# One score group more in a pair, exponentials two by two, and other slots for two batches' side steps

## The chip, the cores and the metric

The kernel runs on one core of a Trainium2 chip. The metric is the time of one execution on the device, in microseconds (us), as the median of several runs. TensorE (PE in the rows, its weight loads PEld) multiplies matrices, ScalarE (ACT) applies functions, VectorE (DVE) and GpSimd (POOL) work elementwise, SyncE (SP) issues most DMAs. Each engine works off its own list of instructions in order; engines wait for one another through semaphores that the language sets.

## The reference

Attention over 4 batches of 12 heads (448 positions, head size 64) with a cap on the scores feeds a mixture of experts: each of the 1792 rows goes to the one expert, of 8, that its gate picks.

```python
scores = scale * q @ k.T                        # per batch and head, 448 x 448
scores = cap * tanh(scores / cap)
attn = exp(scores - max);  attn = attn / (sum(attn) + 1e-9)
x = (attn @ v)  as rows                         # 1792 x 768
logits = x @ w_gate;  e_idx = argmax(logits)
gate_w = softmax(logits)[e_idx];  eom = sigmoid(x @ w_output_gate)
out[rows of e] = gate_w * eom[:, e] * (relu(x[rows of e] @ w1[e]) @ w2[e])
```

## The kernel before, in words

The work has two stages: attention, which ends some 215 us into the profiled execution, and the experts. The change is in the first, and the second is left as it was.

Two heads of a batch are a pair; there are 24 pairs, numbered u = 0 to 23, six to a batch. The loop over u (from line 863) writes for each pair, in this order, what each engine gets:

- `qk(u, s)`, s = 0 to 3: the scores of one block of positions, into one of two PSUM buffers named s. Blocks 0 to 2 are full groups: three products (the high and low parts of k and q, tiles KH, KL, QH, QL), each as two matmuls, one for each head, side by side on the two halves of TensorE's rows. Block 3 is the half group: the 64 remaining positions of both heads as three matmuls on all rows. Behind each group ScalarE applies tanh (line 303, into a tile th, of which there are three).
- The exponential of a group (line 285, into the pair's tile pt) is not put on ScalarE's list with its tanh but one group later: `pend_exp` holds it, and `flush_exp()` in the next `qk` releases it. So tanh and exponential alternate.
- `pv(u - 1, c)`, c = 0 to 3: the previous pair's exponentials times v, into the PSUM tile u (lines 317 and 320).
- `presum(u, .)`: GpSimd adds up a pair's exponentials in three steps (lines 328, 329 and, as two half adds, 333). `sums(u)`: for every other pair TensorE sums them over positions with four matmuls (line 352, tile sm).
- `u_evac` copies a finished pair's result out of PSUM, and `prep(u + 2)` transposes a later pair's k and q (lines 272 and 259, tiles tk and tq), which VectorE then splits into high and low parts.

Between these stand the calls `slot(u, s)` for s = 0, 1, 2, 2.5 and 3. A slot runs the side steps that were put there. When a batch's six pairs are done, its side steps (`end_of_batch`) are spread over the next batch's pairs by the table `at`, whose key x counts slots from pair 6(b+1)+1: x = 5 is slot 1 of the pair after that one, x = 6 its slot 2, and so on. The side steps are: `gate_mm`, `gate_out` (the gate's products on TensorE, lines 389, copied out by ScalarE, line 395, in two halves t[2] and t[3]); `sums_out` (ScalarE copies the sums, line 367, tile ssb); `sums_tr`, `recips` (transposes trec, then VectorE's reciprocals rec, line 377); `gts`, two steps of transposes pg (line 404) and a product by rec (line 411); `logits` and `choose` (VectorE: the best expert); `rank_mm`, `place`, `place2` (TensorE's trk, then VectorE: each row's place in its expert's list); `enter` (VectorE, and then four indirect DMAs from GpSimd, line 474, that scatter the batch's entries into the tables tab); and the six row steps `rws` (transposes trow of one pair, line 483, scaled by VectorE, line 487, and stored to DRAM by a DMA on SyncE's queue, line 490).

All these transposes and products share two PSUM buffers (tag t) with tk and tq: each waits until the buffer of the one before the last has been read.

The batches b = 0 and 1 use one table; batch 2 has its own, with more in a slot, because the experts' first blocks are chosen from it: behind its `enter` come `early`, the weights' first loads, and `gather(0)`, with which the experts begin. Batch 3's steps run in the experts' stage.

Of the kernel before, what the change touches and what calls it, by code (L numbers as in the profile page):

```python
# [21 lines left out]
def tile_kernel(ctx: ExitStack, tc, q, k, v, cap, w_gate, w_ogate, w1, w2, out):  # L22
    nc = tc.nc
    B, H, S, D = q.shape
# [257 lines left out]
    def flush_exp():  # L282
        while pend_exp:
            dst, th = pend_exp.pop(0)
            nc.scalar.activation(out=dst, in_=th, func=ACTF.Exp, scale=capc)  # L285

    def qk(u, s):
        KH, KL, QH, QL = pl[u]
        if s == 0:
            pt[u] = ptp.tile([128, 2 * NK + 1, S], F32, tag="pt", name="pt")  # L290
        n = 2 if s < NK else 1
        sl = slice(s * 128, (s + 1) * 128)
        ps = ps_s.tile([128, 2, 512], F32, tag="s", name="s")
        if s < NK:
            for i, (x, y) in enumerate(((KH, QH), (KL, QH), (KH, QL))):
                for j in range(2):
                    h = slice(64 * j, 64 * j + 64)
                    nc.tensor.matmul(ps[:, j, 0:S], lhsT=x[h, sl], rhs=y[h], start=(i == 0), stop=(i == 2))  # L298
        else:
            for i, (x, y) in enumerate(((KH, QH), (KL, QH), (KH, QL))):  # L300
                nc.tensor.matmul(ps[:, 0, 0:S], lhsT=x[:, sl], rhs=y, start=(i == 0), stop=(i == 2))
        th = thp.tile([128, 2, S], F32, tag="th", name="th")
        nc.scalar.activation(out=th[:, 0:n], in_=ps[:, 0:n, 0:S], func=ACTF.Tanh, scale=icap)  # L303
        flush_exp()
        pend_exp.append((pt[u][:, 2 * s:2 * s + n], th[:, 0:n]))

    def pv(u, c):
        P = pt[u]
        V = vvs[u % 3]
        if c == 0:  # L310
            if u < NU - 1:
                ups[u] = ps_u.tile([128, S], F32, tag="u", name="u")
            else:
                ups[u] = ps_s.tile([128, 2, 512], F32, tag="s", name="u")[:, 0, 0:S]
        if c < NK:
            for j in range(2):
                nc.tensor.matmul(ups[u][64 * j:64 * j + 64], lhsT=V[:, c, j, :], rhs=P[:, 2 * c + j],  # L317
                                 start=(c == 0), stop=False)
        else:
            nc.tensor.matmul(ups[u], lhsT=V[:, c].rearrange("p j d -> p (j d)"), rhs=P[:, 2 * c], start=False, stop=True)  # L320
# [43 lines left out]
    def end_of_batch(b):  # L364
# [130 lines left out]
        rws = [L(P(row_tr, p), P(row_out, p)) for p in range(NP)]  # L495
        t = [sums_out, L(sums_tr, recips), L(P(gate_mm, 0), P(gate_out, 0)), L(P(gate_mm, 1), P(gate_out, 1))]
        gts = [L(P(gate_tr, g), P(gate_mul, g)) for g in range(2)]
        if b < B - 2:
            at = {1: [t[2]], 2: [sums_out], 5: [t[3], t[1]], 6: [rws[0], gts[0]], 10: [rws[1], gts[1]], 11: [logits],
                  12: [choose], 14: [rws[2]], 18: [rank_mm, place, rws[3]], 21: [place2], 23: [enter], 22: rws[4:6]}  # L500
        elif b == B - 2:
            g = early()
            nx = P(next, g, None)
            lds = [P(load_raw, 0, w, c) for w in range(2) for c in range((KD, KF)[w])]
            fd = [P(fetch_dma, i) for i in range(NE)]
            at = {-1: [sums_out], 1: [t[2], t[3]], 2: [t[1], *gts], 3: [logits], 4: [choose],
                  6: [rws[0]], 6.5: [rank_mm, place, place2, enter]}
            for i, x in enumerate(RWP, 1):
                at.setdefault(x, []).append(rws[i])
            for i, x in enumerate(NXP):  # L510
                at.setdefault(x, []).append(nx)
            at[8] = lds[:EL]
            for x, fs in ((9, [fd[0], P(set_known, NE), fd[1]]), (15, [P(gather, 0), fd[2]]), (16, [P(gather, 1), fd[3], *lds[EL:]])):
                at.setdefault(x, []).extend(fs)
# [338 lines left out]
    EARLY = (B - 1) * NP - 1  # L853

    def slot(u, s):
        for f in slots.pop(4 * u + s, ()):
            f()

    for u in range(NU):
        if u > 2:  # L860
            load(u + 3)
        qk(u, 0)
        qk(u, 1)
        if u > 0:
            presum(u - 1, 1)
        slot(u, 0)
        if u > 0:
            pv(u - 1, 0)
            pv(u - 1, 1)
        slot(u, 1)  # L870
        if u in (1, 2):

            prep(u + 1)
            load(u + 3)
        qk(u, 2)
        if u == 0:
            prep(1)
            load(3)
        else:
            pv(u - 1, 2)  # L880
        if u > 1 and u - 2 != EARLY:
            sums(u - 2)
        slot(u, 2)
        qk(u, 3)
        if u > 0:
            pv(u - 1, 3)
            u_evac(u - 1)
        slot(u, 2.5)
        if u > 1:
            prep(u + 2)  # L890
        if u - 1 == EARLY:
            sums(u - 1)
        load_v(u + 2)
        presum(u, 0)
        slot(u, 3)
    u = NU - 1
# [338 lines left out]
```

## Time and profile before

| | us |
|---|---|
| median of 3 runs | 535.86 (535.81 to 539.33) |
| the profiled execution | 536.26 |
| its span in the trace | 534.6 |
| TensorE busy in the span | 512.5 |
| ScalarE | 381.4 |
| VectorE | 339.2 |
| GpSimd | 300.2 |

The page of the profile gives busy time by engine and the costliest groups of instructions. The timeline gives single instructions: start, length, engine, line, what is written from what, and in brackets the idle time of the engine before it and what released it. Matmuls are pipelined and the ends of their rows are modelled, so on TensorE the distance from one row's start to the next is read, not the length. The windows give busy time and TensorE's granted clock (1.00 is full speed, 0.50 half) for chosen stretches. Line numbers are those of the kernel before; from line 304 on the changed kernel's are one higher.

### The profile page before, as it was taken

Reading aid. Unit: us, or ns where it says so; the run is one execution under the profiler, and the core shown is the slowest. Engines: PE = TensorE matmul, PEld = TensorE weight load, DVE = VectorE, ACT = ScalarE, POOL = GpSimd, SP = SyncE. Lnnn points to the kernel's source line nnn. Section 1 sums busy time; section 2 is a strip of 40 time slices with the busy share of each in tenths; the row PEclk is TensorE's granted clock in tenths of the full one; section 3 lists DMA queues with packets and bytes.
Section 4 is the critical chain, followed back from the end, with each engine's and each line's share of the span. In section 5 each row is a group of like instructions: output and inputs, shape, how many; then the busy total and the mean of one; then the engine's idle time right before and its main releaser. Section 6 shows DMA issues by size and latency. Waiting matters only on the chain. (4 is left out here: it accounts for less than half of the span.)

```text
span 534.6 us, 10384 instructions
## 1 busy us (share of the span) xinstructions
PE 512.5 (96%) x3197; PEld 360.2 (67%) x3197; DVE 339.2 (63%) x574; ACT 381.4 (71%) x498; POOL 300.2 (56%) x343
## 2 busy tenths in 40 slices
PE   7999999999999989789999999999999899999993
PEld 6555455555555544367999888887888768676691
DVE  3353356745674783979998896885767766545440
ACT  5988978887888689635678887886767857565550
POOL 8988777877887679725254964314556043331001
PEclk9999999999999899999999999999999999999997
DMA  6653334453445247787159526339759879891001
GB/s 146 141 117 89 87 87 104 103 126 85 103 105 121 52 76 222 260 286 199 61 204 385 215 92 227 107 85 408 240 170 399 321 273 389 281 359 72 1 30 49
DMA packets 106190, 91.95 MB, mean 172 GB/s; under 512 B 80770, under 2 KB 88970, under 8 KB 106128
## 3 DMA queue, kind: packets, MB, share of 16 engines
q1 hardware_dynamic: 97392, 58.48, 37.5%
q0 software_dynamic: 8736, 32.74, 17.1%
q8 instruction: 27, 0.44, 0.3%
q14 instruction: 35, 0.29, 0.2%
HBM read 123.68 MB, written 12.04 MB: 254 GB/s over the span
## 5 line engine op out<-in xcount | busy, mean ns | idle before, releaser
L947 DVE TENSOR_TENSOR wr<-raw,wr 128x768 fp32r<-128x768 f32 (+1 forms) x167 | 171.7, 1067 | 67.1 <-ACT wr L946 59.3
L946 ACT ACTIVATE wr<-raw 128x768 fp32r<-128x768 f32 (+1 forms) x167 | 150.2, 935 | 30.1 <-PE py L968 9.5
L303 ACT ACTIVATE th<-s,icap 128x896 f32<-128x896 f32 x96 | 87.3, 911 | 33.7 <-PE s L298 17.8
L285 ACT ACTIVATE pt<-th,capc 128x896 f32<-128x896 f32 x96 | 90.3, 942 | 0.0
L968 PE MATMUL py<-wr,hh 128*128 128x384 f32 x352 | 77.3, 340 | 0.0
L968 PE MATMUL php<-wr,xh 128*128 128x512 f32 x264 | 74.7, 404 | 0.0
L1037 POOL DMA_INDIRECT out_dram<-yo,ti x13 | 18.1, 1390 | 93.2 <-ACT yo L1035 87.1
L317 PE MATMUL u<-pt,vv 128*64 128x448 f32 x288 | 64.5, 556 | 0.0
L968 PEld LDWEIGHTS py<-wr,hh 128*128 128x128 f32 x352 | 61.2, 188 | 4.0 <-issue 3.7
L328 POOL TENSOR_TENSOR pa<-pt 128x896 f32<-128x896 f32 x23 | 48.4, 2103 | 17.0 <-ACT pt L285 12.2
L968 PEld LDWEIGHTS php<-wr,xh 128*128 128x128 f32 x264 | 47.5, 188 | 12.2 <-issue 2.5
L333 POOL TENSOR_TENSOR pb<-pb,pt 64x448 f32<-64x448 f32 x44 | 50.2, 1141 | 9.5 <-DMA tab<-ent,posi 5.2
L329 POOL TENSOR_TENSOR pb<-pa,pt 128x896 f32<-128x896 f32 x23 | 48.8, 2122 | 4.5 <-POOL pa L328 1.8
L968 PE MATMUL py<-wr,hl 128*128 128x384 f32 x176 | 44.8, 335 | 0.0
L968 PE MATMUL php<-wr,xl 128*128 128x512 f32 x132 | 41.5, 395 | 0.0
L1084 POOL DMA_DIRECT2D rh<-in_moe_w_dram x42 | 23.5, 562 | 24.4 <-DVE wr L947 14.2
L340 DVE COPY ut<-u 128x448 f32<-128x448 f32 x19 | 11.9, 624 | 37.4 <-PE u L320 31.0
L317 PEld LDWEIGHTS u<-pt,vv 128*64 128x64 f32 x288 | 16.5, 135 | 26.4 <-issue 21.2
L298 PE MATMUL s<-QH,KH 64*128 64x448 f32 x144 | 31.7, 437 | 2.3 <-ACT pt L285 1.1
L968 PEld LDWEIGHTS py<-wr,hl 128*128 128x128 f32 x176 | 31.8, 188 | 0.0
L487 DVE TENSOR_TENSOR xr<-trow,rec 112x512 f32<-112x512 f32 x24 | 16.1, 685 | 21.2 <-PE trow L483 18.1
L968 PEld LDWEIGHTS php<-wr,xl 128*128 128x128 f32 x132 | 24.7, 187 | 6.1 <-DVE xl L761 0.2
(243 smaller groups left out, 846.1 us busy)
## 6 DMA issues: line engine op xcount, KB each, us to landing
raw<-in_moe_w_dram SPq DMA_DIRECT2D x78, 512.0 KB
raw<-in_moe_w_dram SPq DMA_DIRECT2D x104, 384.0 KB
rh<-in_moe_w_dram POOLq DMA_DIRECT2D x18, 512.0 KB
rh<-in_moe_w_dram POOLq DMA_DIRECT2D x24, 384.0 KB
lq<-in_q_dram SPq DMA_DIRECT2D x24, 224.0 KB
kk<-in_k_dram SPq DMA_DIRECT2D x24, 192.0 KB
vv<-in_v_dram SPq DMA_DIRECT2D x24, 192.0 KB
xs<-xr SPq DMA_DIRECT2D x18, 224.0 KB
```

Of the source, the lines that this page charges most:

```text
L285: nc.scalar.activation(out=dst, in_=th, func=ACTF.Exp, scale=capc)
L298: nc.tensor.matmul(ps[:, j, 0:S], lhsT=x[h, sl], rhs=y[h], start=(i == 0), stop=(i == 2))
L303: nc.scalar.activation(out=th[:, 0:n], in_=ps[:, 0:n, 0:S], func=ACTF.Tanh, scale=icap)
L317: nc.tensor.matmul(ups[u][64 * j:64 * j + 64], lhsT=V[:, c, j, :], rhs=P[:, 2 * c + j], start=(c == 0), stop=False)
L328: eng.tensor_tensor(out=a, in0=P[:, 0:2], in1=P[:, 2:4], op=ALU.add)
L329: eng.tensor_tensor(out=s1[u], in0=a, in1=P[:, 4:6], op=ALU.add)
L333: eng.tensor_tensor(out=s1[u][h, j], in0=s1[u][h, j], in1=P[h, 2 * NK], op=ALU.add)
L946: nc.scalar.activation(out=t[:, 0, 0:F], in_=raw, func=ACTF.Copy)
L947: nc.vector.tensor_tensor(out=t[:, 1, 0:F], in0=raw, in1=t[:, 0, 0:F].bitcast(F32), op=ALU.subtract)
L968: nc.tensor.matmul(ps[g][:, 0:n], lhsT=st[:, c], rhs=w[:, z, g * n:(g + 1) * n], start=(c == 0 and st is hi and z == 0), stop=(c == (KD, K ...
L1037: nc.gpsimd.indirect_dma_start(out=out, out_offset=bass.IndirectOffsetOnAxis(ap=ti, axis=0), in_=y, in_offset=None, bounds_check=NT - 1, o ...
L1084: nc.gpsimd.dma_start(out=d, in_=src[bass.ds(e, 1)].rearrange("e (k p) f -> p (e k) f", p=128)[:, c], **kw)
```

## The change

It has three parts. First, `flush_exp` now runs only behind the odd groups, s = 1 and s = 3: ScalarE's list has two tanhs, then their two exponentials. Second, in the loop `pv(u - 1, 2)` and `sums(u - 2)` are moved from behind `qk(u, 2)` to the place behind `pv(u - 1, 1)`, so that the half group `qk(u, 3)` follows `qk(u, 2)`, with slot 2 between the two. Third, the table of batches 0 and 1 is written anew: both halves of the gate in one slot, the steps `gts` in slot 1 of their pairs and no longer beside a row step in slot 2, and logits, choose, rank, place and enter some slots later; the last row step of batch 0 has a slot of its own in the next batch's first pair.

```diff
--- before.py
+++ after.py
@@ -301,8 +301,9 @@
                 nc.tensor.matmul(ps[:, 0, 0:S], lhsT=x[:, sl], rhs=y, start=(i == 0), stop=(i == 2))
         th = thp.tile([128, 2, S], F32, tag="th", name="th")
         nc.scalar.activation(out=th[:, 0:n], in_=ps[:, 0:n, 0:S], func=ACTF.Tanh, scale=icap)
-        flush_exp()
         pend_exp.append((pt[u][:, 2 * s:2 * s + n], th[:, 0:n]))
+        if s % 2:
+            flush_exp()
 
     def pv(u, c):
         P = pt[u]
@@ -496,8 +497,9 @@
         t = [sums_out, L(sums_tr, recips), L(P(gate_mm, 0), P(gate_out, 0)), L(P(gate_mm, 1), P(gate_out, 1))]
         gts = [L(P(gate_tr, g), P(gate_mul, g)) for g in range(2)]
         if b < B - 2:
-            at = {1: [t[2]], 2: [sums_out], 5: [t[3], t[1]], 6: [rws[0], gts[0]], 10: [rws[1], gts[1]], 11: [logits],
-                  12: [choose], 14: [rws[2]], 18: [rank_mm, place, rws[3]], 21: [place2], 23: [enter], 22: rws[4:6]}
+            at = {1: [t[2], t[3]], 2: [sums_out], 5: [t[1]], 6: [rws[0]], 9: [gts[0]], 10: [rws[1]], 13: [gts[1]], 14: [rws[2]],
+                  15: [logits], 16: [choose], 18: [rws[3]], 21: [rank_mm, place], 22: [rws[4]], 23: [place2], 24: [enter]}
+            at.setdefault(26 if b < B - 3 else 22, []).append(rws[5])
         elif b == B - 2:
             g = early()
             nx = P(next, g, None)
@@ -867,6 +869,9 @@
         if u > 0:
             pv(u - 1, 0)
             pv(u - 1, 1)
+            pv(u - 1, 2)
+        if u > 1 and u - 2 != EARLY:
+            sums(u - 2)
         slot(u, 1)
         if u in (1, 2):
 
@@ -876,10 +881,6 @@
         if u == 0:
             prep(1)
             load(3)
-        else:
-            pv(u - 1, 2)
-        if u > 1 and u - 2 != EARLY:
-            sums(u - 2)
         slot(u, 2)
         qk(u, 3)
         if u > 0:
```

On TensorE, in pair 4 (tile s are the scores, u the products with v; 64x448 is one head's matmul); lines with - are before, with + after:

```order
 L298 MATMUL s<-QL,KH 128x448 x2
-L317 MATMUL u<-pt,vv_128 64x448 x4
-L298 MATMUL s<-QH,KH 128x448 x2
-L298 MATMUL s<-QH,KL 128x448 x2
-L298 MATMUL s<-QL,KH 128x448 x2
-L317 MATMUL u<-pt,vv_128 64x448 x2
-L301 MATMUL s<-QH,KH 128x448
-L301 MATMUL s<-QH,KL 128x448
-L301 MATMUL s<-QL,KH 128x448
-L320 MATMUL u<-pt,vv_128 128x448
+L318 MATMUL u<-pt,vv_128 64x448 x6
+L298 MATMUL s<-QH,KH 128x448 x2
+L298 MATMUL s<-QH,KL 128x448 x2
+L298 MATMUL s<-QL,KH 128x448 x2
+L301 MATMUL s<-QH,KH 128x448
+L301 MATMUL s<-QH,KL 128x448
+L301 MATMUL s<-QL,KH 128x448
+L321 MATMUL u<-pt,vv_128 128x448
```

The scores stood in three stretches of a pair, parted by products; now they stand in two. Where slot 2 holds a row step, its four transposes stand between the two score groups.

On ScalarE, in pair 13, where batch 1's gate (gsb) and sums (ssb) are copied out; th is a tanh, pt an exponential. Before:

```order
L303 ACTIVATE th<-s,icap 128x896
L285 ACTIVATE pt<-th,capc 128x448
L303 ACTIVATE th<-s,icap 128x896
L285 ACTIVATE pt<-th,capc 128x896
L395 ACTIVATE gsb_1571<-tg 128x448
L303 ACTIVATE th<-s,icap 128x896
L285 ACTIVATE pt<-th,capc 128x896
L367 ACTIVATE ssb<-sm 128x448
L303 ACTIVATE th<-s,icap 128x448
L285 ACTIVATE pt<-th,capc 128x896
```

and now:

```order
L303 ACTIVATE th<-s,icap 128x896 x2
L285 ACTIVATE pt<-th,capc 128x896 x2
L396 ACTIVATE gsb_1570<-tg 128x448
L396 ACTIVATE gsb_1575<-tg 64x448
L303 ACTIVATE th<-s,icap 128x896
L368 ACTIVATE ssb<-sm 128x448
L303 ACTIVATE th<-s,icap 128x448
L285 ACTIVATE pt<-th,capc 128x896
L285 ACTIVATE pt<-th,capc 128x448
```

The second half of the gate came a pair later; now all three copies stand ahead of the pair's last tanh.

On GpSimd, at the scatter of batch 0 (pa and the first pb are a pair's full adds, the pb of 64x448 its two half adds). Before:

```order
L328 TENSOR_TENSOR pa<-pt 128x896
L329 TENSOR_TENSOR pb<-pa,pt 128x896
L474 DMA tab_108<-ent,posi 15488x2
L474 DMA tab_109<-ent,posi 15488x2
L474 DMA tab_110<-ent,posi 15488x2
L474 DMA tab_111<-ent,posi 15488x2
L333 TENSOR_TENSOR pb<-pb,pt 64x448 x2
L328 TENSOR_TENSOR pa<-pt 128x896
```

and now:

```order
L329 TENSOR_TENSOR pa<-pt 128x896
L330 TENSOR_TENSOR pb<-pa,pt 128x896
L334 TENSOR_TENSOR pb<-pb,pt 64x448 x2
L475 DMA tab_108<-ent,posi 15488x2
L475 DMA tab_109<-ent,posi 15488x2
L475 DMA tab_110<-ent,posi 15488x2
L475 DMA tab_111<-ent,posi 15488x2
L329 TENSOR_TENSOR pa<-pt 128x896
```

The scatter stood ahead of pair 12's half adds; now it stands behind them, ahead of pair 13's first full add. Batch 1's moves in the same way, from pair 18's half adds to pair 19's first add. Batch 2's stays where it was, ahead of pair 20's first add.

## Rows read from the trace of the kernel before

**Rows 1.** The page: its first line.

```profile
span 534.6 us, 10384 instructions
```

**Rows 2.** Windows: stretch, length, busy time and count by engine, granted clock, DMA.

```profile
300.00:400.00 100.00, 100.00 (x732) 84.40 (x731) 74.48 (x84) 74.94 (x101) 49.63 (x65) 1.00 0.51 178
...
177.20:180.50 3.30, 3.30 (x15) 2.49 (x15) 1.73 (x3) 1.70 (x3) 3.12 (x2) 0.50 0.17 39
```

**Rows 3.** Timeline, TensorE, pair 6: start, length, line, tiles, count.

```profile
52.35 0.47 PE L298 MATMUL s<-QH,KH 64*128 64x448 f32 x2
53.06 0.37 PE L298 MATMUL s<-QH,KH 64*128 64x448 f32 x2
...
53.77 1.72 PE L317 MATMUL u<-pt,vv 128*64 128x448 f32 x8
55.43 0.47 PE L298 MATMUL s<-QH,KH 64*128 64x448 f32 x2
...
56.23 0.97 PE L317 MATMUL u<-pt,vv 128*64 128x448 f32 x4
57.13 0.47 PE L301 MATMUL s<-QH,KH 128*128 128x448 f32 x1
...
57.85 0.91 PE L320 MATMUL u<-pt,vv 128*128 128x448 f32 x2
```

**Rows 4.** The page's costliest groups: busy, mean ns; idle before, releaser.

```profile
L303 ACT ACTIVATE th<-s,icap 128x896 f32<-128x896 f32 x96 | 87.3, 911 | 33.7 <-PE s L298 17.8
...
L328 POOL TENSOR_TENSOR pa<-pt 128x896 f32<-128x896 f32 x23 | 48.4, 2103 | 17.0 <-ACT pt L285 12.2
...
L333 POOL TENSOR_TENSOR pb<-pb,pt 64x448 f32<-64x448 f32 x44 | 50.2, 1141 | 9.5 <-DMA tab<-ent,posi 5.2
```

**Rows 5.** Timeline, ScalarE, start of pair 6 (in brackets: idle before, releaser).

```profile
53.33 1.01 ACT L303 ACTIVATE th<-s,icap 128x896 f32<-128x896 f32 x1 [0.82 <-PE s L298]
```

**Rows 6.** Timeline, TensorE's weight loads, third score group of pair 6.

```profile
55.43 0.19 PEld L298 LDWEIGHTS s<-QH,KH 64*128 64x128 f32 x2 [0.70 <-ACT pt L285]
```

**Rows 7.** Timeline, TensorE: pair 0, and pair 10's row step.

```profile
10.69 0.66 PE L272 MATMUL tk<-ident,kk 128*128 128x128 f32 x4
11.18 0.55 PE L259 MATMUL tq<-ident,lq 112*128 112x112 f32 x4
...
92.58 0.65 PE L483 MATMUL trow<-ident,ut 128*112 128x128 f32 x4
92.99 0.45 PE L301 MATMUL s<-QH,KH 128*128 128x448 f32 x1
```

**Rows 8.** Timeline around pair 14's start: GpSimd, ScalarE, TensorE.

```profile
120.37 1.17 POOL L333 TENSOR_TENSOR pb<-pb,pt 64x448 f32<-64x448 f32 x1
...
121.62 0.64 ACT L303 ACTIVATE th<-s,icap 128x448 f32<-128x448 f32 x1 [0.97 <-PE tq L259]
...
122.31 0.47 PE L298 MATMUL s<-QH,KH 64*128 64x448 f32 x2 [0.63 <-ACT th L303]
```

**Rows 9.** Timeline in pair 19: GpSimd, TensorE, VectorE.

```profile
171.19 0.95 POOL L474 DMA_INDIRECT tab<-ent,posi  x1 [0.30 <-issue]
172.45 0.96 POOL L474 DMA_INDIRECT tab<-ent,posi  x1 [0.30 <-issue]
...
172.84 0.92 PE L404 MATMUL pg<-ident,gsb 128*112 128x128 f32 x4
...
174.68 0.30 DVE L377 TENSOR_SCALAR rec<-trec,epsc 112x48 f32<-112x48 f32 x1 [6.30 <-PE pg L404]
...
175.04 0.96 PE L404 MATMUL pg<-ident,gsb 128*112 128x128 f32 x4 [1.27 <-DVE rec L377]
```

**Rows 10.** Timeline, from the third scatter to the first expert's transposes.

```profile
189.88 0.96 POOL L474 DMA_INDIRECT tab<-ent,posi  x1 [4.65 <-DVE KL L253]
...
212.88 0.19 POOL L737 TENSOR_TENSOR tc<-tc 128x4 f32<-128x4 f32 x1
...
220.00 0.85 PE L759 MATMUL pt_x<-ident,xg 128*128 128x128 f32 x6 [3.03 <-DMA xg<-xs,ti]
```

## The prediction, made before the result was known

> **What bounds the kernel now.** I read the page first for the span, 534.6 us [rows 1]; the profiled execution took 536.26 us, so 1.66 us lie around the span, and it stands 0.4 us above the median of the runs, 535.86. Then the windows: in the experts' stage TensorE is busy in all 100.00 us of 300 to 400 [rows 2]. What attention gains is carried to the end, as long as the experts can start earlier by as much.
>
> Then TensorE's timeline in one plain pair, 6 [rows 3]. The reader is to see starts that follow one another without a hole, in stretches of scores and stretches of products: TensorE bounds this pair by the length of its list. ScalarE does not: it stands 33.7 us idle ahead of its tanhs, and scores end most of these waits [rows 4]; at pair 6's start it waits 0.82 us [rows 5]. So with the exponentials two by two ScalarE runs the same operations and nothing is gained by that itself.
>
> **The change, part by part.**
>
> *Regrouping on TensorE.* From the starts in [rows 3]: a full score group that ends a stretch takes 53.77 - 53.06 = 0.71, one that begins a stretch takes 53.06 - 52.35 = 0.71, and one that stands alone takes 56.23 - 55.43 = 0.80. Beginning or ending a stretch therefore costs 0.09 each. Two product groups take 55.43 - 53.77 = 1.66, one alone 57.13 - 56.23 = 0.90, so one more behind two costs 0.76, and a stretch of its own 0.14. Before, a pair's middle is score, product, half group, each alone. Now the third product stands behind the first two, and the half group behind the third score group. That saves 0.14 + 0.09 + 0.09 = 0.32 in a pair where slot 2 is empty.
>
> What the saving rests on is seen in the weight loads: at the turn from products to scores the load starts at 55.43, when its matmul starts, after 0.70 idle [rows 6]; it isn't ahead of it. The Trainium skill (TensorE: Matmul & The Clock Gate, Step-by-step: what each phase is for) has the next weights pulled ahead under the running matmul; by that alone turns would be free and this part would save 0. The row differs at these turns, and I go by the row; the other end is a rival below.
>
> Pairs 1 to 6 and 7 have nothing on TensorE in slot 2: 7 x 0.32 = 2.24. In pairs 8 to 20, 13 of them, slot 2 holds row steps, in pair 19 the transposes of sums and gate. There the two score groups stay apart and 0.14 is left, less what the transposes lose by standing behind scores instead of products. Behind products a row step takes 92.99 - 92.58 = 0.41; behind scores the four transposes of pair 0 take 11.18 - 10.69 = 0.49 [rows 7]. These have more columns (128 against 112), so 0.49 bounds the row step from above; from below it is 0.41. A turn of 0.14, as for products, is the far end: 0.55. I take 0.47, nearest the transposes, and 0.08 saved: 13 x 0.08 = 1.04, between 0 and 1.82.
>
> *The products moved ahead.* The third product now needs the pair before's third exponential 0.8 us earlier, but that exponential no longer waits for the next pair's first tanh. It is done early in the pair, where the product starts 3.1 us into it (0.71 + 0.71 + 1.66). This costs nothing. If its cover were gone, it would cost the rest of one exponential. The sums need GpSimd's adds of two pairs ago, a whole pair old: nothing.
>
> *ScalarE.* The score buffer of `qk(u, 2)` waits for the pair's first tanh, that of `qk(u, 3)` for the second. Both now run back to back, and are over three operations of some 0.91 [rows 4] after the start of the first, 0.98 into the pair [rows 5]: by 3.7 us at most, while TensorE comes to `qk(u, 2)` at 0.71 + 0.71 + 1.66 + 0.76 = 3.84. Of the four operations behind them only the tanhs hold TensorE. In pairs 7, 13 and 19 the gate's copies stand ahead of the third tanh (in 7 and 13 the sums' copy too), and wait for the gate's products. ScalarE falls behind by up to three short operations there, and TensorE then needs the third tanh only at the next pair's start, some 3 us after its scores: nothing, or at most 0.6 once or twice.
>
> *The gate's steps.* Moved, not changed: the gate's second half from pair 8 to 7 (14 to 13), the transposes pg from slot 2 to slot 1. They follow products in both places: 0. The row steps' DMAs stay in slot 2, ahead of the next v load on SyncE's queue, as before; batch 0's last moves one pair on, with no reader for 80 us. VectorE's steps move with it, off the path: 0.
>
> *The scatters.* Behind the fourth scatter of a batch two engines stand still. In pair 14 the half add behind it ends at 120.37 + 1.17 = 121.54, ScalarE's last tanh of pair 13 starts at 121.62 and TensorE loses 0.63 [rows 8]. In pair 19 the fourth scatter starts at 172.45; the transposes trec are over when pg starts, at 172.84; VectorE takes them up at 174.68 only. The second pg starts at 175.04, 2.20 after the first, and 1.27 of it idle, as its row says [rows 9]. TensorE then runs from 177.20 to 180.50 with half the clock granted, all 3.30 us of it busy [rows 2]: 1.65 lost. So pair 19 lost 1.27 + 1.65 = 2.92, and pair 14 0.63.
>
> Now both scatters stand behind a pair's half adds, 2 x 1.14 later in GpSimd's list [rows 4], but the exponentials that these adds wait for come earlier. Worked out for pair 19: pair 18's second exponential ends 4.8 into it, its third by 7.3, the adds (2.1 each, half adds 2 x 1.14) are over at 11.7, and pair 18, its steps added up, is about 8.8 long, so the scatters start 2.9 into pair 19, 172.45 - 171.19 = 1.26 apart, and the fourth at 6.7. TensorE reaches trec's end at about the same 6.7. It was 0.39 behind the fourth's start before. That is a margin of 0.4: VectorE has taken up trec before the still stretch, or has not. I take it that it has. For pair 13 the still stretch falls on its last transposes, which wait for no one: 0.63 goes as well.
>
> *Sum.* 2.24 + 1.04 + 0.63 + 2.92 = 6.83; 536.26 - 6.83 = 529.4. Pairs 21 to 23 count for nothing: from the third scatter at 189.88 GpSimd works off its adds up to 212.88, then the first gather, for which TensorE waits 3.03 until 220.00 [rows 10]. What counts is how much earlier pair 20's rank comes.
>
> **The rivals.**
>
> 1. *The margin in pair 19 fails:* the still stretch catches trec again, with the slow clock behind it. For it: 0.4 us is less than I can work out. Then 529.4 + 2.9 = 532.3 (531 to 534).
> 2. *Turns save nothing:* the 0.14 and 0.09 turn up elsewhere, in loads that then stand alone, and only the two stalls go: 536.26 - 0.63 - 2.92 = 532.7. Against it: the late load in [rows 6]. It is the case that the rule above describes.
> 3. *The gain is swallowed at the change of stages:* the wait of 3.03 [rows 10] grows by what attention saves, because something that isn't moved holds the gather: 535.9 to 536.3. Against it: scatter, rows and fetch all follow pair 20's rank.
> 4. *Slower:* the still stretch lasts as long as GpSimd's next operation. In [rows 8] both end together. Behind the moved scatters stands a full add, 2.10, instead of a half add, 1.14 [rows 4]: 0.96 more in pairs 13 and 19. Each would then cost 1.27 + 0.96 + 1.65 = 3.9, both 7.8, and if the clock stays low for two such stretches 5.5 each, 11.0. Against a gain of 2.24 + 1.04 + 0.63 + 2.92 = 6.83 this gives 537.2 to 540.4. It turns slower where the two places cost over 3.4 each. Against it: ScalarE, which has no part in that add's tiles, was held too, so the add alone isn't the cause.
>  The Trainium skill (SBUF — State Buffer, Who interferes with whom) says that a VectorE instruction with two SBUF inputs is fully blocked until a GpSimd one that reads SBUF is over, and that one with at most one such input is not. By it rec, which reads PSUM, would not be held by an add at all, and this rival would fall; the rows show it held, and don't tell by what.
>
> **Numbers.** The forecast of 529.4 has a chance of 0.45 (its own range 527 to 531.5), rival 1 0.27, rival 2 0.10, rival 3 0.09, rival 4 0.09. The range 526.5 to 536.2 takes in the first three and part of the fourth; rival 4 is left out. A measurement of this kernel can tell about 1%, 5.4 us, from no change: faster means under 530.5. That is most of the forecast's case and a little of rivals 1 and 2: 0.44. Slower by over 1%, above 541.2, is the tail of rival 4: 0.04. The rest is 0.52.
>
> **What would show it.** Right: in a plain pair the half group starts some 0.7 behind the third score group, and plain pairs are 0.32 shorter; pg's second step follows the first by under 1 us in pair 19, and the clock stays at 1.00 there; the third scatter starts near 183 and the first expert's transposes near 213. Wrong: an unchanged distance between the starts of plain pairs (rival 2), VectorE's rec over 1 us behind trec (rivals 1 and 4), the gather no earlier though the third scatter is (rival 3). The forecast fails as a whole if ScalarE, not TensorE, sets the pairs' length now: then tanhs would follow one another without idle time and scores would wait for them.

## The result, and the profile after

The changed kernel takes 531.21 us (median of 20 runs) against 537.20 for the kernel before (20 runs beside it): ratio 0.9886, 95% interval 0.9869 to 0.9904, so 5.2 to 7.0 us less. Forecast were 529.4 with a range of 526.5 to 536.2.

The profiled execution of the changed kernel took 534.3 us. Its page begins with this line, 1.9 us below that of before [rows 1]; ScalarE's tanhs wait 26.6 us where they waited 33.7, and GpSimd's half adds 4.4 where they waited 9.5 [rows 4]:

```profile
span 532.7 us, 10341 instructions
...
L303 ACT ACTIVATE th<-s,icap 128x896 f32<-128x896 f32 x96 | 84.2, 914 | 26.6 <-PE s L298 17.7
...
L334 POOL TENSOR_TENSOR pb<-pb,pt 64x448 f32<-64x448 f32 x44 | 50.1, 1139 | 4.4 <-DMA tab<-ent,posi 1.1
```

The 1.9 is the smaller part of what attention gained. The timeline at the change of stages (start, length; in brackets the idle time before and what ended it) has the scatters of batch 2, the first expert's steps on GpSimd, its gather and its transposes:

```profile
184.12 0.96 POOL L475 DMA_INDIRECT tab<-ent,posi  x1 [4.44 <-DVE KL L253]
...
207.07 0.20 POOL L739 TENSOR_TENSOR tc<-tc 128x4 f32<-128x4 f32 x1
...
209.96 1.14 POOL L749 DMA_INDIRECT xg<-xs,ti  x1 [1.45 <-DMA tc<-tab]
...
214.35 0.96 PE L761 MATMUL pt_x<-ident,xg 128*128 128x128 f32 x6 [3.29 <-DMA xg<-xs,ti]
```

Against [rows 10] all of it stands 5.65 to 5.8 us earlier: attention's gain is carried over the change of stages. It stays so up to the transposes that start at 404.31, and at 410.09 before. Then ScalarE's list comes to conversions of weights that have not landed, with the expert's own `h` behind them, and TensorE waits:

```profile
412.95 0.84 ACT L947 ACTIVATE wr<-raw 128x768 fp32r<-128x768 f32 x1 [1.88 <-DMA raw<-in_moe_w_dram]
...
414.76 0.66 PE L761 MATMUL pt_h<-ident,h 128*128 128x128 f32 x4 [2.10 <-ACT h L1030]
```

The next transposes follow 24.09 us later, where they followed after 20.38 before: 3.7 us of the 5.8 are lost here in this execution. The runs' ratio says that most lost less. In the experiments' traces the same stretch took 19.7 to 23.0 us, in no order by how early it began (20.8 in e11, which comes to it first), so here the time differs by some us from one trace to the next.

Now pair 6, TensorE's matmuls and then its weight loads:

```profile
53.83 2.48 PE L318 MATMUL u<-pt,vv 128*64 128x448 f32 x12
56.23 0.47 PE L298 MATMUL s<-QH,KH 64*128 64x448 f32 x2
...
57.04 0.47 PE L301 MATMUL s<-QH,KH 128*128 128x448 f32 x1
...
57.75 0.91 PE L321 MATMUL u<-pt,vv 128*128 128x448 f32 x2
58.50 0.60 PE L272 MATMUL tk<-ident,kk 128*128 128x128 f32 x4
```

```profile
56.23 0.19 PEld L298 LDWEIGHTS s<-QH,KH 64*128 64x128 f32 x2 [0.70 <-ACT pt L285]
...
57.04 0.19 PEld L301 LDWEIGHTS s<-QH,KH 128*128 128x128 f32 x1 [0.31 <-issue]
...
57.56 0.39 PEld L321 LDWEIGHTS u<-pt,vv 128*128 128x128 f32 x2
```

Three products take 56.23 - 53.83 = 2.40, where two and one took 1.66 + 0.90 [rows 3]. The third score group takes 0.81 and the half group behind it 0.71: as much as each took alone. So the pair is 7.01 long, 0.16 less than before, and not 0.32. The loads show where the rest went: the half group's load starts with its matmul (57.04, after 0.31 idle), so there is a turn ahead of it still; the last product's starts 0.19 ahead of its matmul (57.56 and 57.75). Scores have weights of 64 x 128, products 128 x 64, and the half group, the last product and the transposes tk 128 x 128. The load runs ahead where this shape stays the same, and not where it changes among these three. (The transposes tq, 112 x 128, follow tk without a turn: their load starts at 58.83, their matmul at 58.94.)

And pair 19: two of the four scatters and the add behind them, TensorE, VectorE, and the window of the pair (length; busy time and count of TensorE, its loads, VectorE, ScalarE, GpSimd; granted clock, DMA):

```profile
168.14 0.96 POOL L475 DMA_INDIRECT tab<-ent,posi  x1 [1.35 <-DVE ent L473]
...
171.93 0.95 POOL L475 DMA_INDIRECT tab<-ent,posi  x1 [0.30 <-issue]
172.94 2.12 POOL L329 TENSOR_TENSOR pa<-pt 128x896 f32<-128x896 f32 x1
```

```profile
169.09 0.65 PE L373 MATMUL trec<-ident,ssb 128*112 128x128 f32 x4
169.58 1.81 PE L405 MATMUL pg<-ident,gsb 128*112 128x128 f32 x8
```

```profile
169.78 0.31 DVE L378 TENSOR_SCALAR rec<-trec,epsc 112x48 f32<-112x48 f32 x1 [2.46 <-issue]
```

```profile
162.80:173.70 10.90, 10.90 (x71) 5.89 (x67) 6.63 (x19) 7.80 (x10) 8.42 (x8) 1.00 0.43 97
```

Against [rows 9]: both steps of pg follow one another without a hole, VectorE takes up trec 0.69 behind its start, TensorE is busy in all 10.90 us of the window, and the clock that stood at 0.50 behind the stall [rows 2] stays at 1.00. The pair is 10.86 long, where it took 13.42.

### The profile page after: what moved, and what is told of

It is laid out like the page before. It is cut to its first block, busy times and chain, and to the rows that moved or that the text cites. A ratio compares the mean times of both kernels' runs of the same rounds, so it can differ in the third digit from the quotient of the medians.

```text
span 532.7 us, 10341 instructions
## 1 busy us (share of the span) xinstructions
PE 510.4 (96%) x3197; PEld 363.3 (68%) x3197; DVE 343.7 (65%) x574; ACT 381.9 (72%) x498; POOL 300.0 (56%) x343
## 3 DMA queue, kind: packets, MB, share of 16 engines
HBM read 123.68 MB, written 12.04 MB: 255 GB/s over the span
## 5 line engine op out<-in xcount | busy, mean ns | idle before, releaser
L303 ACT ACTIVATE th<-s,icap 128x896 f32<-128x896 f32 x96 | 84.2, 914 | 26.6 <-PE s L298 17.7
L285 ACT ACTIVATE pt<-th,capc 128x896 f32<-128x896 f32 x96 | 85.7, 947 | 0.0
L318 PE MATMUL u<-pt,vv 128*64 128x448 f32 x288 | 59.4, 548 | 0.1
L318 PEld LDWEIGHTS u<-pt,vv 128*64 128x64 f32 x288 | 18.5, 136 | 30.2 <-issue 23.1
L298 PE MATMUL s<-QL,KH 64*128 64x448 f32 x144 | 26.9, 365 | 0.0
```

## The experiments

The table has for each run the time from pair 0's first scores to the first expert's transposes in its trace, against 212.35 before and 206.55 with the change, and the ratio of its runs to the kernel before, timed beside it.

| run | first scores to transposes | against before | ratio, 95% interval |
|---|---|---|---|
| the change | 206.55 | -5.80 | 0.9886 (0.9869 to 0.9904) |
| e1, loop alone | 211.43 | -0.92 | 0.9996 (0.9963 to 1.0029) |
| e2, exponentials alone | 215.56 | +3.21 | 1.0082 (1.0053 to 1.0110) |
| e3, table alone | 208.23 | -4.12 | 0.9908 (0.9877 to 0.9940) |
| e4, half group behind the last product | 206.32 | -6.03 | 0.9923 (0.9897 to 0.9949) |
| e5, old rank and scatters | 214.31 | +1.96 | 1.0001 (0.9971 to 1.0031) |
| e6, change with old exponentials | 206.94 | -5.41 | 0.9859 (0.9842 to 0.9876) |
| e7, pair 22's adds on VectorE | 207.93 | -4.42 | 0.9895 (0.9870 to 0.9920) |
| e8, all small steps | 205.47 | -6.88 | 0.9893 (0.9871 to 0.9914) |
| e9, before with the scatters moved | 208.70 | -3.65 | 0.9916 (0.9887 to 0.9945) |
| e10, change with the scatters back | 212.08 | -0.27 | 0.9958 (0.9938 to 0.9978) |
| e11, rows first | 201.96 | -10.39 | 0.9820 (0.9790 to 0.9851) |

### The three parts, one by one

e1 moves the product and the sums in the loop:

```diff
             pv(u - 1, 1)
+            pv(u - 1, 2)
+        if u > 1 and u - 2 != EARLY:
+            sums(u - 2)
         slot(u, 1)
...
-        else:
-            pv(u - 1, 2)
-        if u > 1 and u - 2 != EARLY:
-            sums(u - 2)
```

> Only the product and the sums are moved; exponentials and table as before. The prediction's reckoning (a score stretch costs 0.09 at each end, a product stretch of its own 0.14): plain pairs 6.85 us instead of 7.17, the time 3.3 us less than before. Rival, from the changed kernel's rows: a turn costs 0.15 wherever the matmuls change their tile shape (scores 64x128, products 128x64, half group, last product and transposes 128x128), whatever they compute: one turn less in a pair, plain pairs 7.02, the time some 2.5 to 3 us less. Both leave pair 14's and pair 19's stalls (0.6 and 2.9 us) where they are, since the scatters are not moved.

Plain pairs take 7.01 and 7.90 to 7.93, as the rival had it, and pairs 9 to 12 and 15 to 18 are 0.13 to 0.17 shorter each. Pair 19's stall is gone (10.85), which neither expected, and other pairs pay for it: pair 14 takes 13.66 instead of 10.86, pair 20 10.05 instead of 8.85, pair 2 8.69 instead of 8.14. GpSimd and ScalarE in pair 14:

```profile
119.70 1.17 POOL L333 TENSOR_TENSOR pb<-pb,pt 64x448 f32<-64x448 f32 x1
124.84 1.14 POOL L333 TENSOR_TENSOR pb<-pb,pt 64x448 f32<-64x448 f32 x1 [3.98 <-DMA tab<-ent,posi]
```

```profile
126.02 1.04 ACT L285 ACTIVATE pt<-th,capc 128x896 f32<-128x896 f32 x1 [2.80 <-POOL pb L333]
```

The second half add behind the scatters waits until they have landed, and the exponentials, whose buffer it reads, wait for it. The wait was in the trace of before too, in pair 14 and in pair 19, though there ScalarE's exponentials followed one another without idle time and no one paid for it. The prediction did not use it:

```profile
123.97 1.14 POOL L333 TENSOR_TENSOR pb<-pb,pt 64x448 f32<-64x448 f32 x1 [2.44 <-DMA tab<-ent,posi]
...
177.30 1.13 POOL L333 TENSOR_TENSOR pb<-pb,pt 64x448 f32<-64x448 f32 x1 [2.74 <-DMA tab<-ent,posi]
```

e2 changes the order of the exponentials alone:

```diff
-        flush_exp()
         pend_exp.append((pt[u][:, 2 * s:2 * s + n], th[:, 0:n]))
+        if s % 2:
+            flush_exp()
```

> Only the order of tanhs and exponentials is changed. The prediction: ScalarE does not bound a pair, so plain pairs stay at 7.17 and the time is that of before within 0.5 us, with pair 19's stall of 2.9 still there. Rival: the earlier exponentials bring GpSimd's adds and with them the scatters forward, and the stall goes by this alone: 3 us less than before. Second rival: the last tanh of a pair now holds the next pair, 0.2 to 0.5 us in each: 4 to 10 us more.

Plain pairs stay at 7.17 and 8.04, so the order holds nothing in a pair. But pair 14 takes 13.53: the same half add waits 4.37, and ScalarE's exponentials 3.38 for it. Pairs 10 and 16 lose 1.15 and 0.77, since the transposes tq wait for a buffer, and pairs 2 and 20 0.45 and 0.56. Pair 19's stall is gone here too (11.02), although the scatters stand where they stood and trec is over 0.49 behind the fourth one's start, as late as before (0.39):

```profile
177.19 0.95 POOL L475 DMA_INDIRECT tab<-ent,posi  x1 [0.30 <-issue]
...
177.68 0.47 PE L405 MATMUL pg<-ident,gsb 128*112 128x128 f32 x2
...
177.88 0.30 DVE L378 TENSOR_SCALAR rec<-trec,epsc 112x48 f32<-112x48 f32 x1 [4.76 <-PE trec L373]
```

VectorE takes trec up 0.20 behind its end. So how trec stands to the fourth scatter does not decide alone whether the stall comes. In sum 3.2 us are lost in the trace, and 2.8 to 5.9 in the runs. None of the three expectations had this cause.

e3 takes over the new table `at` for batches 0 and 1, and nothing else.

> Only the places of the gate, rank and row steps of batches 0 and 1 are changed. The prediction: plain pairs stay at 7.17; the stalls of pairs 14 and 19 go with the moved scatters, 3.55 us less than before. Rival: the places alone do nothing, because the adds that the scatters stand behind come as late as before, and one of the stalls is only moved: within 1 us of before.

As the prediction has it, with more: 4.1 us less in the trace. Pair 14's and pair 19's stalls are gone.

### The scatters alone

```diff
-                  12: [choose], 14: [rws[2]], 18: [rank_mm, place, rws[3]], 21: [place2], 23: [enter], 22: rws[4:6]}
+                  12: [choose], 14: [rws[2]], 18: [rank_mm, place, rws[3]], 21: [place2], 24: [enter], 22: rws[4:6]}
```

> The kernel before with one step moved: the four scatters of batches 0 and 1 go behind the next pair's two half adds on GpSimd's list (enter from 23 to 24); no other engine's list changes. If the scatters' place is what pairs 14 and 19 lost, as the prediction has it: 3.55 us less, the first expert's transposes near 216 instead of 220, 532 to 533 us against 537. If the other moved steps carry it: within 1 us of before. If a full add behind the scatters, instead of a half add, lengthens the still stretch (the prediction's slower rival): 1 to 5 us more than before.

Pair 14 takes 9.95 instead of 10.86, pair 19 11.00 instead of 13.42, pair 20 8.62 instead of 8.85: 3.56 less together, and the other pairs up to 22 are as before within 0.02. The prediction had worked out 3.55. A full add now follows the scatters and costs nothing. In pair 19 trec is now over 2.2 us ahead of the fourth scatter, and pg runs through:

```profile
174.30 0.95 POOL L474 DMA_INDIRECT tab<-ent,posi  x1 [0.30 <-issue]
```

```profile
172.09 1.81 PE L404 MATMUL pg<-ident,gsb 128*112 128x128 f32 x8
173.83 0.47 PE L301 MATMUL s<-QH,KH 128*128 128x448 f32 x1
```

From pg's start to the half group 1.74 us pass here, and 3.09 passed before (172.84 to 175.93), so the stall was 1.35. From the last product on, before, every step up to pair 20's second score group took longer at the granted clock of 0.50; against e9 that is 1.59. Together this is 2.94. Pair 20 loses 0.30 anew in e9, where its transposes tk wait for VectorE. In pair 14 the first score group took 1.51 before instead of 0.71, and the second, alone behind the stall, 0.80 instead of 0.71:

```profile
120.80 0.47 PE L298 MATMUL s<-QH,KH 64*128 64x448 f32 x2
...
123.11 1.72 PE L317 MATMUL u<-pt,vv 128*64 128x448 f32 x8
```

e5 and e10 put the scatters back into the changed kernel. e5 has the rank and its place back as well:

```diff
-                  15: [logits], 16: [choose], 18: [rws[3]], 21: [rank_mm, place], 22: [rws[4]], 23: [place2], 24: [enter]}
+                  15: [logits], 16: [choose], 18: [rank_mm, place, rws[3]], 21: [place2], 22: [rws[4]], 23: [enter]}
```

> The changed kernel, with the rank, place and table steps of batches 0 and 1 where they were: the four scatters stand ahead of a pair's two half adds again, and all else is changed. Theory from the single parts: the second half add behind the scatters waits until they have landed; with only one half add (1.14 us) between, it waits 2 to 4.4 us again, the exponentials two pairs later wait for it, and pairs 14 and 20 lose 2.5 to 3.6 us each: 536 to 538 us against 531.2. The prediction's theory: what counts is whether rec is taken up before the still stretch behind the fourth scatter; pair 19 loses up to 2.9 us and pair 14 nothing: 534 us. If the scatters' place is not the cause at all: 531 us.

Most of its loss is another one: choose stands only two slots ahead of the rank here, and the rank's matmul waits 1.96 and 1.75 for VectorE, so pairs 11 and 17 lose 3.2 and 3.0 us. Pair 14 loses nothing although the half add waited 2.05, pair 20 loses 0.57, where it waited 4.44, and pair 19 loses 1.18, where pg's second step waits 1.10. The time is the one that the first theory gave, and for the greater part not for its reason. As a test of the scatters' place this run is muddied, and e10 leaves rank and place where the change has them:

```diff
-                  15: [logits], 16: [choose], 18: [rws[3]], 21: [rank_mm, place], 22: [rws[4]], 23: [place2], 24: [enter]}
+                  15: [logits], 16: [choose], 18: [rws[3]], 21: [rank_mm, place], 22: [place2, rws[4]], 23: [enter]}
```

> The changed kernel with only the scatters of batches 0 and 1 put back ahead of a pair's half adds (enter from 24 to 23, place2 one place earlier so that it can); rank and place stay where the change put them. If the scatters' place carries the gain: 1 to 4 us more than the changed kernel (pair 19's second step of the gate waits 1.1 as in the run with the old places, or up to 2.9), 532 to 535. If it was the rank's wait in pairs 11 and 17 alone that cost the run with the old places its 6 us: 531 us.

5.5 of the 5.8 us are gone, but not where it was expected. Pair 19 has no stall (10.88). Pairs 12 and 18 lose 1.0 and 1.6, where place2 now stands ahead of a row step on VectorE; this is a price of place2, not of the scatters. Pair 20 loses 3.1. There the half add waits 4.29 for the landing, GpSimd's next adds come as much later, and they meet VectorE's steps of choose:

```profile
177.89 1.14 POOL L334 TENSOR_TENSOR pb<-pb,pt 64x448 f32<-64x448 f32 x1 [4.29 <-DMA tab<-ent,posi]
179.11 2.11 POOL L329 TENSOR_TENSOR pa<-pt 128x896 f32<-128x896 f32 x1
```

```profile
179.91 1.36 DVE L422 TENSOR_TENSOR d<-lg,mx 112x32 f32<-112x32 f32 x1
181.31 2.13 DVE L543 SCALAR_TENSOR_TENSOR cand<-d,iota 112x32 f32<-112x32 f32 x1
```

```profile
184.69 0.18 PE L438 MATMUL trk<-ohb,tri 112*112 112x32 bf16 x1 [2.11 <-DVE ohb L431]
```

In the changed kernel the same two steps take 0.84 and 1.18 in pair 20. So the scatters' old place had two prices: TensorE's work is taken up late behind the fourth (before, and e5), and the second half add waits for the landing, which either holds ScalarE (e1, e2) or brings adds over VectorE's work (e10). Of the five traces with the scatters in their old place, pair 19 has its stall in two (before and e5) and not in three (e1, e2, e10). Which price TensorE pays is a matter of where it stands, and so is not to be summed up part by part.

### What a turn costs

e4 sets the half group behind the last product, and releases the exponentials from the second group on:

```diff
-        if s % 2:
+        if s:
             flush_exp()
...
-        qk(u, 3)
         if u > 0:
             pv(u - 1, 3)
+        qk(u, 3)
+        if u > 0:
             u_evac(u - 1)
```

> The changed kernel with the half group behind the pair's last product instead of behind the third score group, and that group's exponential ahead of the half group's tanh. By the prediction's reckoning a score stretch more, so 2 x 0.09 = 0.18 more in a plain pair (7.19 instead of 7.01), 3 to 4 us more than the changed kernel. By the rival (a turn where the tile shape changes): the last product then pays the turn and the half group behind it none, so plain pairs stay at 7.01, half group 0.56 instead of 0.71, and the time is that of the changed kernel within 0.5 us.

Plain pairs take 7.01 and 7.89 to 7.90: the rival's figure. Pair 6:

```profile
57.16 0.47 PE L298 MATMUL s<-QH,KH 64*128 64x448 f32 x2
...
57.97 1.02 PE L321 MATMUL u<-pt,vv 128*128 128x448 f32 x2
58.48 0.71 PE L301 MATMUL s<-QH,KH 128*128 128x448 f32 x1
...
59.43 0.60 PE L272 MATMUL tk<-ident,kk 128*128 128x128 f32 x4
```

Third score group 0.81, last product and half group together 59.43 - 57.97 = 1.46, as 0.71 + 0.75 in the changed kernel. A score stretch more costs nothing. What counts is the change of the weights' shape: both orders have four of these in a pair and take 7.01, the kernel before has five and takes 7.17. The 0.15 is what one less saved; the rows do not price each of them by itself.

### The exponentials and the end of attention

e6 is the changed kernel with `flush_exp()` where it was before.

> The changed kernel with the exponentials one by one as before; product, sums and table stay changed. If the places of the steps carry the gain and one turn less (0.15 in a pair) is the rest: 531.2 us as the changed kernel, 0.6 less if pair 2 gets its stall back from the constant's step. If the exponentials two by two are needed for the moved product (ScalarE is late by 0.1 to 0.5 in a pair without them, as pairs 4 to 8 of the run with the loop alone show): 1 to 3 us more, 532 to 534.

The trace loses 0.4 us against the changed kernel, and the runs are if anything shorter (the intervals overlap): with loop and table changed, exponentials two by two are worth nothing that can be measured. Pair 2 keeps its stall (8.67), and pairs 11 and 17 take 8.28 instead of the changed kernel's 8.72 and 8.73.

e7 takes pair 22's full adds off GpSimd, whose work the prediction held to be what the first gather waits for:

```diff
-        eng = nc.vector if u == NU - 1 or (u, s) == (NU - 2, 1) else nc.gpsimd
+        eng = nc.vector if u >= NU - 2 else nc.gpsimd
```

> The changed kernel with the two full adds of pair 22 on VectorE instead of GpSimd. By the prediction GpSimd works without pause from batch 2's scatters to the first gather, so the gather starts 4.5 us earlier and TensorE's wait for the first expert's tokens (3.29 us at 214.35) goes nearly whole: first transposes near 211, 528 us against 531.2. Rivals: VectorE, with the adds in its list, holds the last pairs by as much, or the gather then waits for the rows of batch 2: 530 to 533.

GpSimd is through 4.0 us earlier, and the gather starts when it did (209.96 in the changed kernel); it lasts 2.13 instead of 1.14, and the transposes even start 1.36 later (215.71):

```profile
203.01 1.52 POOL L742 TENSOR_SCALAR ti<-tb 128x1 uint32<-128x1 f32 x1
209.84 2.13 POOL L749 DMA_INDIRECT xg<-xs,ti  x1 [5.31 <-DMA tc<-tab]
```

It waits for DMAs, as in the changed kernel (1.45). Before, it had done so too, for 1.44 us, which [rows 10] leave out:

```profile
215.76 1.15 POOL L747 DMA_INDIRECT xg<-xs,ti  x1 [1.44 <-DMA tc<-tab]
```

e8 adds four steps, each for a stall that the changed kernel's trace shows:

```diff
-    slots.setdefault(9, []).append(eps)
+    slots.setdefault(11, []).append(eps)
-                  15: [logits], 16: [choose], 18: [rws[3]], 21: [rank_mm, place], 22: [rws[4]], 23: [place2], 24: [enter]}
+                  15: [logits], 18: [rws[3], choose], 21: [rank_mm, place], 22: [rws[4]], 23: [place2], 24: [enter]}
-    NXP = (7, 7, 7, 7, 7, 7)
+    NXP = (7, 7, 7, 7, 7, 10)
-            for x, fs in ((9, [fd[0], P(set_known, NE), fd[1]]), (15, [P(gather, 0), fd[2]]), (16, [P(gather, 1), fd[3], *lds[EL:]])):
+            for x, fs in ((11, [fd[0], P(set_known, NE), fd[1]]), (15, [P(gather, 0), fd[2]]), (16, [P(gather, 1), fd[3], *lds[EL:]])):
```

> As the run before, and: the constant's step behind pair 2's transposes (0.6 us less if it is what holds pair 2), choose behind the row step of pairs 11 and 17 (0.6 each), the last of the early steps and the fetch behind the two row steps of pair 21 (1.4 us less). If each stall is TensorE's own loss and the gather keeps ahead: 3.2 us less than the run before, 524.8. If GpSimd's list sets the experts' start again, only what comes ahead of pair 20's rank is left, 1.8 less: 526. If the stalls only move: 528.

Pair 2 takes 7.99 instead of 8.62, pairs 11 and 17 8.28 instead of 8.72, pair 21 9.33 instead of 10.47: each stall goes, 2.7 us in all. But the gather, at 208.40, still waits 3.99 for DMAs, and TensorE 3.87 for it, so of this 1.1 are left against the changed kernel at the first transposes, and none in the runs (0.9893 and 0.9886). All three times that were expected were too low. SyncE's queue shows what comes last: the three rows of batch 2 (xs) are issued behind eight fetches of the token table (tc), although VectorE had the first ready at 196.4:

```profile
196.80 5.19 SPq L734 DMA_DIRECT2D tc<-tab  x8
202.10 1.99 SPq L491 DMA_DIRECT2D xs<-xr  x3
```

e11 is e8 with the rows ahead:

```diff
-    RWP = (10, 10, 14, 14, 14.5)
+    RWP = (10, 10, 12, 13, 14)
-            for x, fs in ((11, [fd[0], P(set_known, NE), fd[1]]), (15, [P(gather, 0), fd[2]]), (16, [P(gather, 1), fd[3], *lds[EL:]])):
+            for x, fs in ((13, [fd[0], P(set_known, NE)]), (15, [P(gather, 0), fd[1], fd[2]]), (16, [P(gather, 1), fd[3], *lds[EL:]])):
```

> As the run with all small steps, and batch 2's last three row steps 1, 2 and 2.5 places earlier, with the first fetch of the token table between them and the second fetch behind them. The first gather waited 4 to 5 us for DMAs although GpSimd had been through its adds; the last of these are the rows' writes, issued by SyncE behind eight fetches. If the rows hold the gather: it starts near 205.5 instead of 208.4, the first expert's transposes near 210, 3 us less than the run before, 526 to 528 us. If the fetch itself holds it: transposes unchanged near 213, 530 to 531 us. In both the late weights of an expert at 405 to 415 us can take back up to 4 us.

525.95 us, ratio 0.9820 (0.9790 to 0.9851) to the kernel before, 1.5 to 2.1% less; the changed kernel's interval, from other runs, lies above this one. The fetches of the token table went later and the rows earlier, so the rows, as they stood, held the gather; whether the fewer fetches ahead of it had a part in the gain is not told apart. It starts at 204.57, and TensorE goes over from attention's last product to the first expert without a wait of note:

```profile
204.57 1.70 POOL L749 DMA_INDIRECT xg<-xs,ti  x1 [0.48 <-DMA tc<-tab]
```

```profile
208.75 1.02 PE L321 MATMUL u<-pt,vv 128*128 128x448 f32 x2
209.61 0.82 PE L761 MATMUL pt_x<-ident,xg 128*128 128x128 f32 x6
```

## Why the prediction was right, point by point

The forecast of 529.4 was 0.3% below the median; by the ratio, 536.26 x 0.9886 = 530.1. The sum came out nearly right with several of its terms wrong, and that they cancelled was luck. Measured in the traces, from the first scores to the first expert's transposes:

| step | forecast | measured | shown by |
|---|---|---|---|
| turns, pairs 1 to 7 | 2.24 | some 1.0 (0.15 in a pair) | e1, e4 |
| turns, pairs 8 to 20 | 1.04 | some 2.0 (0.15 in a pair) | e1 |
| scatters, pairs 14 and 19 (with 20) | 3.55 | 3.56 | e9 |
| gate's and row steps moved | 0 | 1.0 up to pair 23's start | e3 against e9 |
| pair 2 | 0 | -0.6 | e8 |
| pairs 11 and 17 | 0 | -0.9 | e8 |
| change of stages | 0 | -0.3 | 6.07 gained at pair 23's start, 5.80 at the transposes |
| sum | 6.83 | 5.8; the traces' difference is 5.80 | |

**Turns.** The size was nearly right in sum and its reason wrong. The prediction priced the ends of score stretches (0.09) and stretches of products (0.14) from where they stood, and so had 0.32 in a plain pair and 0.08 in one with a row step. Its 0.14 for the product stretch held (2.40 instead of 1.66 + 0.90). Its 0.09 + 0.09 came to nothing, because the third score group and the half group, though side by side, differ in the shape of their weights and took as long as alone. The 0.06 that it took off for a row step came to nothing too. One change of shape less, worth 0.15, is left in every pair, plain or not, and the two errors nearly cancelled: 7 x 0.17 too much, 13 x 0.07 too little. The Trainium skill (TensorE: Matmul & The Clock Gate, Step-by-step: what each phase is for) says that the next weights are pulled ahead under a running matmul if row groups don't conflict or the background buffer is loaded. The trace agrees between groups of one shape (57.56 ahead of 57.75) and differs where the shape changes (57.04). Rival 2, turns that save nothing, is out by e1: 0.15 in each pair.

**Scatters.** Moving them brought the gain: e9 moves nothing else and has 3.56. That the stalls came of their place alone is not shown, for e1 and e2 lost pair 19's stall with the scatters in the old place. The working was off at two points. The scatters did not wait for the adds but for VectorE's entry ([1.35 <-DVE ent]), so they started 5.3 us into pair 19, not 2.9. With that trec was over 2.3 us ahead of the fourth scatter's start (169.58 and 171.93), where the prediction had the two together with 0.4 to spare: rival 1 did not come near, by luck, because of a wait that the prediction left out. And by e2 such a margin need not decide. The size agrees in part by luck. Pair 19's stall and the slow clock behind it were read rightly (2.92; 2.94 measured, with part of it in pair 20). Pair 14 lost 0.9, not 0.63: the prediction took the idle time of the row, which hangs on a modelled end, instead of the distance of the starts. And 0.3 that pair 20 loses anew made up for this. Rival 4, a still stretch as long as the add behind the scatters, is refuted: in the changed kernel ScalarE goes on at 122.58, in the middle of a full add that lasts from 121.58 to 123.68, and e9 loses nothing by the longer add.

**ScalarE and the exponentials.** "Nothing is gained by that itself" holds (e6). That it costs nothing does not: alone it costs 3.2 us in the trace (e2), because adds that come earlier or later meet the landing elsewhere, and with the rest changed it costs 0.9 in pairs 11 and 17, which e6 has back and loses again in other places.

**Steps counted at nothing.** In pair 2 the constant's step on ScalarE (line 161) now stands behind two exponentials, VectorE's step behind it runs 0.85 later (26.30 instead of 25.45), with the splits behind that, and the transposes wait for their buffer; e8 moves the step and has the 0.63 back. The two exponentials are not the only way to this: with them one by one (e1, e6) the step came late as well, and pair 2 took 8.69 and 8.67. In pairs 11 and 17 choose's step cand, which takes 0.19 us by itself (in pair 10 before), starts behind a full add of GpSimd's and lasts until that is over, and the row behind it, with its buffer, waits:

```profile
98.94 2.11 POOL L329 TENSOR_TENSOR pa<-pt 128x896 f32<-128x896 f32 x1
```

```profile
99.02 2.08 DVE L543 SCALAR_TENSOR_TENSOR cand<-d,iota 112x32 f32<-112x32 f32 x1
```

Both are covers that the prediction named for other steps and did not look up for these. The moved gate and row steps, counted at nothing, gave back 1.0 by pair 23's start. A part of it is seen: the gate's halves side by side take 1.63 us in e3, apart they took 0.89 + 0.88. The rest is not taken apart by any run.

**The change of stages.** Rival 3 did not happen: by the trace's clock attention had gained 5.92 at pair 23's start, and 5.65 of it is there at the first transposes. But the reason given, GpSimd without pause up to the first gather, is not what held the gather, which waited 1.44 for DMAs behind GpSimd's last step. e7 took pair 22's adds away and gained nothing; e11 brought the rows forward on SyncE's queue and gained 3.5 us on e8 at the transposes. GpSimd's list and the DMAs ended within 1.5 us of one another, and both had moved with the pairs. That attention's gain is carried to the end holds by the runs' ratio (6.1 us), and not in every execution: the profiled one lost 3.7 us of it at 404 to 428 us, where weights landed late, and the prediction had no term for this.

## What to carry to other kernels

Try a step that scatters at other places in its engine's list, and see what waits for its landing and what is taken up late behind it; here that one place, of all that the change moved, was worth 3.6 of 5.8 us, and the other two parts alone were worth nothing that the runs show, or less. Count turns of TensorE by the shape of the weights, not by what is computed, and put equal shapes side by side. See which of VectorE's small steps with two inputs will fall under an add of GpSimd's. A part that is harmless or useful with the others can cost us alone when two waits stand close together, so single parts don't add up: read which wait each of them met.

## What the runs showed of the hardware

One change of the weights' shape less in a pair saved TensorE 0.15 us (e1), in either of two orders (e4). Between a half group and a product, both of 128 x 128, the load ran ahead of its matmul.

Behind the last of four scatters other engines took up TensorE's finished work late. In the kernel before, the last product in pair 13 was over at 120.05 and the transposes tk at 120.5, and SyncE, VectorE and ScalarE [rows 8] went on together:

```profile
121.59 1.12 SPq L113 DMA_DIRECT2D vv<-in_v_dram  x2
```

```profile
121.60 0.62 DVE L340 COPY ut<-u 128x448 f32<-128x448 f32 x1 [6.47 <-PE tq L259]
```

In the trace's semaphore events six of TensorE's updates stand between 121.53 and 121.80, one upon the other. In the changed kernel a tanh waited 1.71 us at 122.58 in the same way, under a stretch of products that hid it. What holds the updates stays open: each time the fourth scatter had ended 1.0 to 1.3 us before, but behind batch 1's in the changed kernel and in e2 (pair 19) nothing of the kind is seen (in the changed kernel VectorE takes up tk at 173.43, as soon as it is over).

VectorE's step cand, which has two inputs in SBUF, lasted until the GpSimd add that it fell under was over. It took 0.19 us where none ran:

```profile
93.01 0.19 DVE L541 SCALAR_TENSOR_TENSOR cand<-d,iota 112x32 f32<-112x32 f32 x1
```

In pair 11 of the changed kernel it took 2.08, from 99.02 to 101.10, under an add that ended at 101.05. The Trainium skill (SBUF — State Buffer, Who interferes with whom) says that a VectorE instruction with two SBUF inputs contends with a GpSimd instruction that reads SBUF. The trace agrees.

The half adds that waited for the scatters' landing started 4.0 to 9.2 us behind the fourth one's start (e1 and e6; 4.6 and 4.9 before). The first gather started 4.6 us behind the end of SyncE's issue of batch 2's last rows in the changed kernel (205.3 and 209.96), and 4.3 in e8.
